# Seven second products from layer 2's first block pair on, and a second weight that is converted and summed within layer 1

## The chip, the cores and the metric

The kernel runs on one core of a Trainium2 chip. The metric is the device time of one execution in microseconds (us). Engines are named as in the profile: PE is TensorE (PEld its weight loads), DVE VectorE, ACT ScalarE, POOL GpSimd, SP the engine that issues most DMAs.

## The reference

A channel attention over 6016 tokens of 256 channels, then two dense layers with a hidden width of 2048:

```
s = kn.T @ qn / tau;  a = softmax(s);  x = v @ a          # a is 256 x 256
h = x @ w_in;   g = h * clip(h + 3, 0, 6) / 6;  x = g @ w_out      # layer 1
h = max(x @ w_in2, 0);  out = (h * h) @ w_out2                      # layer 2
```

The weights are 256 x 2048 and 2048 x 256 and come as 64-bit words. Inputs x, q, k and v and the output are float32.

## The kernel before

**Products.** All values are kept to float32 by splitting each operand into a high and a low part of a shorter type (`F32R`). One product of a 128 x 128 weight block with up to 512 tokens is therefore three matmuls: high x high, low x high, high x low.

**Tiling.** Tokens run along the free axis. They are cut into six block pairs (`pairs`), five of 2 x 512 and one of 2 x 448 tokens. The hidden width is cut into eight groups (`g`) of 2 x 128. `groups` lists layer, pair and group in the order of work: 2 x 6 x 8 = 96; groups 0 to 47 are layer 1, 48 to 95 layer 2. In a group, the first weight (2 x 2 blocks) meets the tokens (2 x 2 blocks), the result goes through the nonlinear function, and its split parts (`g` or `gs`) meet the second weight (2 x 2 blocks again). A 2 x 2 block product takes eight products in the plain way, or seven by sums of operands.

**Two schemes.** In the older one, `first7` does the first product in seven products and `second` the second product in eight, so a group has 21 + 24 = 45 matmuls; `hidden` does the nonlinear function and the split; results add up in four PSUM banks (`acc`). In the newer one, `first7s` does the first product in seven, and `items_direct` and `items_t` the second in seven, 42 matmuls. For this, sums of the hidden values are needed: `chain` adds two on VectorE and hands others to accumulating DMAs on GpSimd's queue (`move`, L1692), and `split_t` splits them three groups later. The second weight needs sums of its blocks too: `sums2` forms them from a converted block, four of 128 x 128, and splits them (`w2x`). Before the change, the newer scheme holds for layer 2 from its second pair on (`by7`, `S2SET`), except the last two groups of all, and group 56 is its first.

**Weights.** A second weight's block is loaded raw and converted by `pair_of`: six instructions on VectorE, two on ScalarE. Within layer 1, other work runs beside the groups, as listed in a table of group numbers: `make_w1` converts and sums layer 2's first weight and stores it to DRAM, `make_wo2` converts blocks 0 to 3 of its second weight and stores them (`wo2_d`). `load_wo2` brings those back once layer 1 is done with the buffer; blocks 4 to 7 are loaded raw and converted into their place (`need_wo(1, late)`) at the layer border. `sums2` runs in the eight groups of layer 2's first pair, one block each, in buffers that the layer-1 work has given up (`extra_cells`). First weights are loaded two groups ahead from DRAM, three buffers in turn (`load_w1`); from the newer scheme on, such a load also waits until a `move` has landed.

**Order.** Nothing is issued directly: each step is an `Op` with an engine, a cost, a delay and dependencies. PE and DMA operations keep the order in which the program adds them. For DVE, ACT and POOL, `Plan.run` picks by a rank: the latest time by which an operation must start for PE not to wait. `blame` raises ranks where the planned PE idles, for operations from `plan.settled` on. All SP transfers share one queue, and a transfer that waits holds up those behind it.

Of the kernel before, what the change touches and what calls it, by code (L numbers as in the profile page):

```python
# [196 lines left out]
def tile_kernel(  # L197
# [54 lines left out]
    PLAIN = 1  # L252

# [541 lines left out]
    def tokens(l, pr, parts=False):  # L795
# [696 lines left out]
    S2SET = {pr: tuple(range(NG if pr < NP - 1 else NG - 2)) for pr in range(1, NP)}  # L1492
    S2ALL = sorted({g for gs in S2SET.values() for g in gs})
    S2AT = {g: g + 3 for g in range(NG)}

    def by7(l, pr, g):
        return l == 1 and g in S2SET.get(pr, ())

# [24 lines left out]
    def sums2(k, g):  # L1523

        t, free = {}, cv_r.take()
        p = wo[1, g]

        def f_a():
            em = cv_p.tile([P, 2, 512], F32, tag="em", name="a2")
            t["a"], t["s"] = em[:, 0], em[:, 1].rearrange("p (k n) -> p k n", n=P)  # L1530
            V.tensor_tensor(
                t["a"], p["hl"][:, :512].bitcast(F32), p["hl"][:, 512:].bitcast(F32), ALU.add
            )

        def a(e, i):
            c = i * C + e * P
            return t["a"][:, c : c + P]

        def f1():
            V.tensor_tensor(t["s"][:, 0], a(1, 0), a(1, 1), ALU.subtract)  # L1540

        def f2():
            V.scalar_tensor_tensor(t["s"][:, 1], t["s"][:, 0], -1.0, a(0, 1), ALU.mult, ALU.subtract)

        def f3():
            V.tensor_tensor(t["s"][:, 2], a(0, 1), a(1, 1), ALU.subtract)

        def f4():
            V.tensor_tensor(t["s"][:, 3], a(0, 0), t["s"][:, 1], ALU.add)

        cell = cells["x", k]

        def f_hi():
            A.activation(cell.ap()[:, 0], t["s"], AF.Copy)

        def f_lo():
            x = cell.ap()
            V.tensor_tensor(x[:, 1], t["s"], x[:, 0].bitcast(F32), ALU.subtract)

        c = dve_us(P)  # L1560
        o = ordered("cv", add("DVE", dve_us(512), f_a, wo_done[1, g], free))
        wo_held[1, g].append(o)
        s1 = add("DVE", c, f1, o)
        s2 = add("DVE", c, f2, s1)
        s3 = add("DVE", c, f3, o)
        s4 = add("DVE", c, f4, s2)
        hi = add("ACT", act_us(512), f_hi, s3, s4, cell.take())
        lo = add("DVE", dve_us(512), f_lo, hi)
        cv_r.reader(lo)
        w2x[g], w2x_done[g] = cell, (hi, lo)  # L1570

    def extra_cells():
        deps = all_of(op8_r)
        for k in range(2):
            cells["x", k] = Cell(lambda: pools["op8"].tile([P, 2, 4, P], F32R, tag="op8", name="w2x"), deps)
        deps = all_of(wA_r)
        for k in range(2, 6):
            cells["x", k] = Cell(lambda: wA.tile([P, 2, 4, P], F32R, tag="wA", name="w2x"), deps)

        for k in (6, 7):  # L1580
            cells["x", k] = Cell(lambda k=k: more_p.tile([P, 2, 4, P], F32R, tag=f"w2x{k}", name="w2x"))
# [41 lines left out]
    def first7s(pr, g):  # L1623

        l, n = 1, pairs[pr][1]
# [5 lines left out]
        u = {"n": n, "pr": pr, "g": g, "seven": seven, "R": R}  # L1631
# [139 lines left out]
    def second_of(u, bank, operand, w, w_ok, first=None, last=True):  # L1771

        n, (c, hi, lo) = u["n"], operand
        key = (u["pr"], bank)
# [3 lines left out]
        held = wo_held[1, u["g"]]  # L1778
# [48 lines left out]
    def items_t(u):  # L1827
        g = u["g"]
        return (
            lambda: second_of(u, "P7", u["t3"], w_sum(g, 2), w2x_done[g]),  # L1830
            lambda: second_of(u, "P6", u["t2"], w_sum(g, 1), w2x_done[g]),
            lambda: second_of(u, "P4", u["t4"], w_plain(g, 1, 0), wo_done[1, g]),
        )

    def items_direct(u):
        g, ok = u["g"], wo_done[1, u["g"]]
        return (
            lambda: second_of(u, "P2", u[3], w_plain(g, 0, 0), ok),
            lambda: second_of(u, "P3", u[2], w_sum(g, 3), w2x_done[g]),
            lambda: second_of(u, "P1", u[1], w_plain(g, 0, 1), ok),  # L1840
            lambda: flush(u, "f5", second_of(u, "Y", u["t1"], w_sum(g, 0), w2x_done[g], first=True)),
        )

    def items_plain(u):
        g, ok = u["g"], wo_done[1, u["g"]]

        def unit(k, e, bank, **kw):
            return lambda: second_of(u, bank, u[k], w_plain(g, e, ROW[k]), ok, **kw)
# [16 lines left out]
    def out_s(pr, e, b, src, op, held):  # L1865
        o, n = pairs[pr]

        queue = nc.scalar if pr == NP - 1 and e == b else nc.sync

        def f_st():  # L1870
            c = o + b * n
            queue.dma_start(outT[e * P : (e + 1) * P, c : c + n], src()[:, :n])

        def store():
            held.append(add("DMA", 0.73, f_st, op, lat=5.0))

        if pr == NP - 1:
# [13 lines left out]
    def dve_out(pr, dst, a, b, op, deps, order=None):  # L1891
        n = pairs[pr][1]
# [7 lines left out]
    def finish_a(pr):  # L1900
        n = pairs[pr][1]
# [21 lines left out]
    def finish_b(pr):  # L1923
# [8 lines left out]
        n = pairs[pr][1]  # L1932
# [17 lines left out]
    def finish_last(pr, z):  # L1950
        s1, f5, fz = cells["s1"], cells["f5"][pr % 2], cells["fz"]
        n = pairs[pr][1]
# [29 lines left out]
    groups = [(l, pr, g) for l in range(2) for pr in range(NP) for g in range(NG)]  # L1982

# [3 lines left out]
    for i, job in (  # L1987
        (16, ("w1", 0)), (20, ("wo2", 0)), (22, ("w1", 1)), (27, ("wo2", 1)), (29, ("w1", 2)),
        (34, ("wo2", 2)), (36, ("w1", 3)), (41, ("wo2", 3)),
    ):  # L1990
# [13 lines left out]
    for i, (l, pr, g) in enumerate(groups):  # L2004
        if l == 0 and pr == 0:
            stores.pop(0)()
        k = i - (NP + 1) * NG
# [12 lines left out]
        for _ in range(1 if l and pr else len(pending)):  # L2020
# [20 lines left out]
        if g == (0 if l else 2) and i + NG < len(groups):  # L2041
            x_load = tokens(*groups[i + NG][:2], l == 1 and pr > 0)
            if not (l and pr):
                list(x_load)
        if l and pr and g < 7 and pr < NP - 1:
# [11 lines left out]
        if k >= 0:  # L2057
            steps, us[k] = first7s(pr, g)
# [10 lines left out]
            elif d:  # L2069
# [4 lines left out]
                if (pr, g) == (NP - 1, NG - 1):  # L2074
# [39 lines left out]
    finish_last(pr, x[7])  # L2114
# [3 lines left out]
    finish_rest(pr)  # L2118
# [48 lines left out]
```

## Time and profile before

| | |
|---|---|
| time, median of 3 runs | 1019.07 us (1018.51 to 1019.6) |
| profiled execution | 1017.72 us, its span 1015.8 us |
| PE busy | 1007.2 us, 4508 matmuls |
| DVE / ACT / POOL busy | 886.8 / 791.6 / 100.4 us |
| DMA | 188.73 MB, mean 186 GB/s |
| granted clock | 1.00 |

The span runs from the first to the last instruction. A busy PE is not a PE at its peak, since the rows of neighbouring matmuls overlap; its turn is the distance from one start to the next. Layer 2's first pair runs from 547.3 to 628.39 us, and the newer scheme's first matmul is at 628.39 us.

### The profile page before, as it was taken

What the parts mean: (1) busy time and instruction counts of PE and PEld (TensorE: products, weight loads), DVE (VectorE), ACT (ScalarE), POOL (GpSimd) and SP (SyncE); (2) the same over time, 40 slices, a digit from 0 to 9 for tenths busy, and PEclk for the clock granted to TensorE, in tenths of its full rate; (3) what the DMA queues carried; (4) which work ended last, traced back from release to release, by engine and by line L of the source; (5) the groups of instructions that cost most, each with busy time, mean ns of one, the idle gap of its engine ahead of it and who ended that gap; (6) DMA issues with size and microseconds to landing.
All of it is one profiled execution on the core that took longest, in us unless ns stands there. A gap on an engine that the chain in (4) does not pass through costs nothing.

```text
span 1015.8 us, 12950 instructions
## 1 busy us (share of the span) xinstructions
PE 1007.2 (99%) x4508; PEld 842.7 (83%) x4508; DVE 886.8 (87%) x1350; ACT 791.6 (78%) x1190; POOL 100.4 (10%) x97
## 2 busy tenths in 40 slices
PE   9999999999999999999999999999999999999998
PEld 7888888888888888888998888888888788888897
DVE  3999987988989899799788998789999889999886
ACT  5787667677778778777767888889889788888884
POOL 3400000000000000000000000122222222222220
PEclk9999999999999999999999999999999999999999
DMA  9657536536463744653755423697997888897892
GB/s 363 268 177 247 151 120 196 193 130 215 148 207 114 244 135 134 219 171 126 252 195 195 145 75 118 173 219 170 223 220 182 186 225 197 194 231 196 189 221 70
DMA packets 70208, 188.73 MB, mean 186 GB/s; under 512 B 7296, under 2 KB 11648, under 8 KB 68864
## 3 DMA queue, kind: packets, MB, share of 16 engines
q1 hardware_dynamic: 54048, 158.16, 46.3%
q0 software_dynamic: 15808, 29.30, 17.2%
q8 instruction: 35, 0.57, 0.2%
q10 hardware_dynamic: 288, 0.46, 0.1%
q14 instruction: 29, 0.24, 0.1%
HBM read 126.35 MB, written 32.24 MB: 156 GB/s over the span
## 4 chain that ended last, share of the span: by engine, by line
PE 81%; DMA 10%; issue 4%; DVE 3%; POOL 1%; ACT 0%; SPq 0%; DVEq 0%; POOLq 0%
PE acc L1419 9%; PE acc L1420 9%; PE acc L1425 9%; PE A L1327 4%; PE xy L1640 4%; PE A L1328 4%; PE A L1326 4%; PE xy L1642 4%; PE xy L1641 4%; PE s L958 3%; DMA rs<-rs 3%; DMA rc<-rc 2%; PE acc L1783 2%; PE acc L1784 2%; PE acc L1785 2%
## 5 line engine op out<-in xcount | busy, mean ns | idle before, releaser
L1419 PE MATMUL acc<-g,wo 128*128 128x512 f32 (+1 forms) x448 | 172.9, 386 | 0.0
L1420 PE MATMUL acc<-g,wo 128*128 128x512 f32 (+1 forms) x448 | 172.9, 386 | 0.0
L1208 ACT ACTIVATE g<-r 128x1024 fp32r<-128x1024 f32 (+1 forms) x112 | 117.1, 1046 | 46.1 <-DVE r L1182 45.2
L1212 DVE TENSOR_TENSOR g<-r,g 128x1024 fp32r<-128x1024 f32 (+1 forms) x112 | 135.0, 1206 | 20.0 <-ACT g L1208 19.3
L1425 PE MATMUL acc<-g,wo 128*128 128x512 f32 (+1 forms) x448 | 136.6, 386 | 0.0
L1420 PEld LDWEIGHTS acc<-g,wo 128*128 128x128 f32 x448 | 84.1, 188 | 16.2
L1419 PEld LDWEIGHTS acc<-g,wo 128*128 128x128 f32 x448 | 84.1, 188 | 16.2
L1425 PEld LDWEIGHTS acc<-g,wo 128*128 128x128 f32 x448 | 84.1, 188 | 16.1
L1692 POOL DMA_DIRECT2D rs<-rs x20 | 21.2, 1060 | 665.4 <-DVE gs L1676 619.4
L1177 ACT ACTIVATE r<-hp,three 128x1024 f32<-128x1024 f32 (+1 forms) x40 | 45.3, 1132 | 43.8 <-DVE hp L1359 43.5
L1351 ACT ACTIVATE hp<-A 128x512 f32<-128x512 f32 (+1 forms) x96 | 56.6, 590 | 12.9 <-PE A L1328 11.9
L1640 PE MATMUL xy<-xt,w 128*128 128x512 f32 (+1 forms) x160 | 62.4, 390 | 0.0
L1642 PE MATMUL xy<-xt,w 128*128 128x512 f32 (+1 forms) x160 | 61.6, 385 | 0.0
L1641 PE MATMUL xy<-xt,w 128*128 128x512 f32 (+1 forms) x160 | 61.6, 385 | 0.0
L1182 DVE SCALAR_TENSOR_TENSOR r<-r,hp 128x1024 f32<-128x1024 f32 (+1 forms) x40 | 47.9, 1198 | 14.8 <-ACT r L1177 14.3
L1359 DVE TENSOR_TENSOR hp<-B,hp 128x512 f32<-128x512 f32 (+1 forms) x48 | 32.6, 680 | 20.5 <-PE B L1328 15.0
L1640 PE MATMUL xy<-xb,w 128*128 128x512 f32 (+1 forms) x120 | 46.4, 387 | 0.7 <-ACT hs L1665 0.6
L1783 PE MATMUL acc<-gs,wo 128*128 128x512 f32 (+1 forms) x122 | 46.9, 384 | 0.0
L1785 PE MATMUL acc<-gs,wo 128*128 128x512 f32 (+1 forms) x122 | 46.9, 384 | 0.0
L1784 PE MATMUL acc<-gs,wo 128*128 128x512 f32 (+1 forms) x122 | 46.9, 384 | 0.0
L1676 DVE TENSOR_TENSOR gs<-rs,gs 128x512 fp32r<-128x512 f32 (+3 forms) x50 | 43.7, 880 | 3.4 <-ACT gs L1671 3.0
L1642 PE MATMUL xy<-xb,w 128*128 128x512 f32 (+1 forms) x120 | 46.2, 385 | 0.0
(388 smaller groups left out, 2776.4 us busy)
## 6 DMA issues: line engine op xcount, KB each, us to landing
w<-w1d SPq DMA_DIRECT2D x176, 448.0 KB, 4.4
qk<-in_qk_dram SPq DMA_DIRECT2D x8, 1024.0 KB, 16.6
w1d<-wA SPq DMA_DIRECT2D x16, 448.0 KB, 5.6
xr<-in_vT_dram SPq DMA_DIRECT2D x5, 1024.0 KB, 7.2
x2d<-o SPq DMA_DIRECT2D x20, 256.0 KB, 3.5
w1d<-wA SPq DMA_DIRECT2D x16, 256.0 KB, 2.5
rs<-rs POOLq DMA_DIRECT2D x8, 512.0 KB, 6.1
rp<-rp POOLq DMA_DIRECT2D x8, 512.0 KB, 6.1
```

Source lines behind the costliest of these rows:

```text
L1208: A.activation(t["g"][:, a:b, 0, :n], t["t"][:, a:b, :n], AF.Copy)
L1212: V.tensor_tensor(g[:, a:b, 1, :n], t["t"][:, a:b, :n], g[:, a:b, 0, :n].bitcast(F32), ALU.subtract)
L1351: A.activation(dst(), t[bank][:, :n], AF.Copy)
L1419: T_.matmul(acc[b, e][:, :n], w(e, 0), gh_, start=first_of, stop=False)
L1420: T_.matmul(acc[b, e][:, :n], w(e, 1), gh_, start=False, stop=False)
L1425: T_.matmul(acc[b, e][:, :n], w(e, 0), gl_, start=False, stop=last_of_b)
L1640: T_.matmul(ps, wh, xh, start=start, stop=False, skip_group_check=True)
L1641: T_.matmul(ps, wl, xh, start=False, stop=False, skip_group_check=True)
L1642: T_.matmul(ps, wh, xl, start=False, stop=True, skip_group_check=True)
L1783: T_.matmul(ps, wh, gh, start=first, stop=False, skip_group_check=True)
L1784: T_.matmul(ps, wl, gh, start=False, stop=False, skip_group_check=True)
L1785: T_.matmul(ps, wh, gl, start=False, stop=last, skip_group_check=True)
```

## The change

The newer scheme starts with layer 2 (`FIRST = (1, 0, 0)`), at group 48 instead of 56. All eight blocks of layer 2's second weight are now converted within layer 1 (`JOBS`, groups 13 to 39 instead of 16 to 41), stored, and loaded back at groups 42 to 49. The sums of blocks 0 to 3 are formed right after their conversion, from the converted block and before it is given up; those of blocks 4 to 7 at groups 48 to 51, two groups after their load, the last three of them in the buffers `fz` and `s1`. `sums2` now works in place, in half a buffer. Tokens of layer 2's second pair come in four pieces. Functions of the newer scheme get the layer as an argument, so that the pair's number counts through both layers. `SOME` is empty: layer 1 stays as it was.

```diff
+    FIRST = (1, 0, 0)
+    JOBS = (
+        (13, ("w1", 0)), (16, ("wo2", 0)), (18, ("wo2", 1)), (20, ("w1", 1)), (23, ("wo2", 4)),
...
+    GAP = 2
@@ make_wo2
+        if i < 4:
+            if i == 2:
+                extra_cells((2, 3), op8_p, "op8", op8_r)
+            sums2(1, i, (p, (hi, lo), wA_held))
@@ tokens
-        for k in (1, 0, 3, 2) if l and pr else range(4):
+        for k in (1, 0, 3, 2) if fast(l, pr) else range(4):
@@
-    S2SET = {pr: tuple(range(NG if pr < NP - 1 else NG - 2)) for pr in range(1, NP)}
+    groups = [(l, pr, g) for l in range(2) for pr in range(NP) for g in range(NG)]
+    K0 = groups.index(FIRST)
+    LAG = 3
     def by7(l, pr, g):
-        return l == 1 and g in S2SET.get(pr, ())
+        if groups.index((l, pr, g)) < K0:
+            return False
+        return g in SOME if l == 0 else pr < NP - 1 or g < NG - 2
@@ sums2
-    def sums2(k, g):
+    def sums2(l, g, early=None):
+        (p, ready, read), held = early or (wo[l, g], wo_done[l, g], wo_held[l, g]), []
+        if "fz" in cells:
+            tmp = cells[("fz", "s1")[g % 2]]
+        else:
+            tmp = Cell(lambda: cv_p.tile([P, 2, 512], F32, tag="em", name="a2")[:, 0], cv_r.take())
@@ the loop over groups
-        k = i - (NP + 1) * NG
+        k = i - K0
-        late = i - (NP - 1) * NG - 2
-        if 0 <= late < NG // 2:
+        late = i - (NP - 1) * NG - (2 if K0 == NP * NG else 4)
+        if 0 <= late < NG:
             load_wo2(late)
-        elif NG // 2 <= late < NG:
-            need_wo(1, late)
-        if -NG <= k < 0:
-            if k == -NG:
-                extra_cells()
-            if k == -6:
-                plan.settled = len(plan.ops)
-            sums2(k + NG, S2ALL[k + NG])
+        if k == -5:
+            extra_cells(range(4, NG), wA, "wA", wA_r)
+        if k == -6:
+            plan.settled = len(plan.ops)
+        if 4 <= late - GAP < NG:
+            sums2(1, late - GAP)
```

PE at the layer border, from the last product of layer 1's last group (`A057`) on. Before, the older scheme goes on with layer 2's first group:

```order
L1328 MATMUL A057_4766<-xb22_4147,w1_4617 128x448
L1326 MATMUL A100_4854<-xb11_4488,w1_4693 128x512
L1327 MATMUL A100_4854<-xb11_4488,w1_4693 128x512
L1328 MATMUL A100_4854<-xb11_4488,w1_4693 128x512
L1326 MATMUL C100_4862<-xb21_4510,w1_4693 128x512
L1327 MATMUL C100_4862<-xb21_4510,w1_4693 128x512
L1328 MATMUL C100_4862<-xb21_4510,w1_4693 128x512
```

After, the newer scheme (`xy` banks) starts there, with the second products of layer 1's last group (`acc05..`) between:

```order
L1340 MATMUL A057_4853<-xb22_4233,w1_4701 128x448
L1661 MATMUL xy_4941<-xb11_4655,w1_4780 128x512
L1662 MATMUL xy_4941<-xb11_4655,w1_4780 128x512
L1663 MATMUL xy_4941<-xb11_4655,w1_4780 128x512
L1431 MATMUL acc0500_4363<-g_4935,wo07_1267 128x448
L1432 MATMUL acc0500_4363<-g_4935,wo07_1267 128x448
L1661 MATMUL xy_4957<-xb21_4660,w1_4780 128x512
L1662 MATMUL xy_4957<-xb21_4660,w1_4780 128x512
L1663 MATMUL xy_4957<-xb21_4660,w1_4780 128x512
```

Up to that row PE's order is the same in both, and in all it has 4373 rows before and 4349 after.

SP in the middle of layer 1, where blocks of the second weight pass (`wo21r` is block 1 raw, `wo2d1` its store; `w1` from `w1d..` the first weights of a coming group, `win2..` raw first weights of layer 2). Before:

```order
L330 DMA wo21r_3110<-in_w_out2_dram 128x512
L585 DMA w1_3158<-w1d06_115 128x896 x2
L585 DMA w1_3241<-w1d07_116 128x896 x2
L500 DMA wo2d1_102<-wA_3214 128x1024
L330 DMA win220r_3281<-in_w_in2_dram 128x512
L330 DMA win221r_3289<-in_w_in2_dram 128x512
L585 DMA w1_3322<-w1d00_109 128x896 x2
L585 DMA w1_3408<-w1d01_110 128x896 x2
```

After, blocks 4 and 5 pass in about the same groups, and block 1 has had its turn earlier:

```order
L508 DMA wo2d4_105<-wA_3074 128x1024
L338 DMA wo25r_3101<-in_w_out2_dram 128x512
L597 DMA w1_3119<-w1d04_113 128x896 x2
L814 DMA xr04_3138<-in_vT_dram 128x2x1024
L597 DMA w1_3157<-w1d05_114 128x896 x2
L508 DMA wo2d5_106<-wA_3204 128x1024
L338 DMA win220r_3255<-in_w_in2_dram 128x512
L338 DMA win221r_3269<-in_w_in2_dram 128x512
L597 DMA w1_3282<-w1d06_115 128x896 x2
L597 DMA w1_3303<-w1d07_116 128x896 x2
L597 DMA w1_3370<-w1d00_109 128x896 x2
```

There are now eight such stores instead of four, each with first weights of coming groups behind it, and SP has 294 rows for 283 in all.

DVE in layer 2's first pair before, where sums (`a2`, L1531 to L1549) and their low parts (`w2x`, L1558) stand between the steps of a group (`hp`, `h`, `r`, `g`):

```order
L1531 TENSOR_TENSOR a2_5313<-wo2_4602 128x512
L1359 TENSOR_TENSOR hp_5319<-C105_5315,hp_5319 128x512
L1540 TENSOR_TENSOR a2_5313<-a2_5313 128x128
L1531 TENSOR_TENSOR a2_5333<-wo3_4639 128x512
L1212 TENSOR_TENSOR g_5328<-r_5288,g_5328 128x2x512
L1543 SCALAR_TENSOR_TENSOR a2_5313<-a2_5313 128x128
L1546 TENSOR_TENSOR a2_5313<-a2_5313 128x128
L1549 TENSOR_TENSOR a2_5313<-a2_5313 128x128
L1540 TENSOR_TENSOR a2_5333<-a2_5333 128x128
L1558 TENSOR_TENSOR w2x_5349<-a2_5277,w2x_5349 128x512
L1359 TENSOR_TENSOR hp_5319<-B105_5323,hp_5319 128x512
```

DVE after, around the newer scheme's first totals (`ISA`), with the sums of block 4 and the low part of block 3 between:

```order
L1194 SCALAR_TENSOR_TENSOR r_4928<-r_4928,h_4888 128x448
L1224 TENSOR_TENSOR g_4935<-r_4913,g_4935 128x2x448
L1194 SCALAR_TENSOR_TENSOR r_4928<-r_4928,A057_4853 128x448
L1556 TENSOR_TENSOR a2_4955<-wo4_4803 128x512
L1561 TENSOR_TENSOR a2_4955<-a2_4955 128x128
L1679 ISA rs_4951<-xy_4957,rs_4951 128x512
L1224 TENSOR_TENSOR g_4961<-r_4928,g_4961 128x2x448
L1564 TENSOR_TENSOR a2_4955<-a2_4955 128x128
L1579 TENSOR_TENSOR w2x_4675<-a2_4575,w2x_4675 128x512
L1679 ISA rs_4973<-xy_4941,rs_4973 128x512
L1567 SCALAR_TENSOR_TENSOR a2_4955<-a2_4955 128x128
```

The sums of blocks 0 to 3 have been formed in layer 1 by then, and the totals and splits of the newer scheme stand where the older scheme's steps were.

## Rows read from the trace of the kernel before

**Rows 1.** The page, busy us (share of the span) and instructions by engine.

```profile
PE 1007.2 (99%) x4508; PEld 842.7 (83%) x4508; DVE 886.8 (87%) x1350; ACT 791.6 (78%) x1190; POOL 100.4 (10%) x97
```

**Rows 2.** TensorE's waits, whole span: us in total, times, longest.

```profile
PE xy L1640 <- ACT hs L1665: 0.6, 1, 0.6
PE A L1327 <- DMA w<-w1d: 0.2, 1, 0.2
```

**Rows 3.** TensorE's timeline, first matmul of groups: start us, us.

```profile
556.99 0.39 PE L1326 MATMUL A<-xb,w 128*128 128x512 f32 x1
...
567.19 0.39 PE L1326 MATMUL A<-xb,w 128*128 128x512 f32 x1
...
720.85 0.39 PE L1640 MATMUL xy<-xb,w 128*128 128x512 f32 x1
...
730.37 0.39 PE L1640 MATMUL xy<-xb,w 128*128 128x512 f32 x1
```

**Rows 4.** Stretches: length, then busy us by engine, in three pairs of each layer.

```profile
core 0: us, PE busy (x) PEld busy (x) DVE busy (x) ACT busy (x) POOL busy (x), PEclk, DMA share, GB/s
227.20:309.00 81.80, 81.80 (x363) 67.73 (x362) 72.71 (x107) 61.17 (x86) 0.00 (x0) 1.00 0.52 177
309.00:391.00 82.00, 82.00 (x364) 67.89 (x363) 75.43 (x110) 62.49 (x87) 0.00 (x0) 1.00 0.49 164
391.00:473.00 82.00, 82.00 (x364) 67.94 (x363) 73.56 (x112) 60.77 (x85) 0.00 (x0) 1.00 0.49 162
547.30:628.39 81.09, 81.09 (x362) 67.55 (x360) 74.70 (x131) 68.26 (x97) 0.00 (x0) 1.00 0.38 129
628.39:704.70 76.31, 76.31 (x335) 61.96 (x334) 63.93 (x89) 66.98 (x107) 13.98 (x13) 1.00 0.77 191
704.70:781.10 76.40, 76.40 (x338) 62.84 (x337) 70.31 (x101) 66.47 (x104) 16.84 (x16) 1.00 0.86 203
```

**Rows 5.** VectorE's instructions of one conversion and of the sums: min/median/max ns.

```profile
L391 DVE TENSOR_SCALAR em<-wo23r x1: 416/416/416, 499.8 to 499.8; 128x512 uint32<-128x512 uint32 x1
...
L412 DVE SCALAR_TENSOR_TENSOR em<-wo23r,em x1: 684/684/684, 504.5 to 504.5; 128x512 f32<-128x512 uint32 x1
...
L1531 DVE TENSOR_TENSOR a<-wo x8: 680/684/685, 565.8 to 615.0; 128x512 f32<-128x512 f32 x8
...
L1546 DVE TENSOR_TENSOR a<-a x8: 282/284/287, 571.7 to 620.8; 128x128 f32<-128x128 f32 x8
```

**Rows 6.** VectorE's timeline, two neighbours.

```profile
791.40 0.68 DVE L1676 TENSOR_TENSOR gs<-rs,gs 128x512 fp32r<-128x512 f32 x1
792.00 0.69 DVE L1676 TENSOR_TENSOR gs<-hs,gs 128x512 fp32r<-128x512 f32 x1
```

**Rows 7.** ScalarE's and TensorE's timeline around the one loss in layer 2.

```profile
804.95 1.06 ACT L1671 ACTIVATE gs<-rs 128x1024 fp32r<-128x1024 f32 x1 [2.35 <-DMA rs<-rs]
...
797.20 0.39 PE L1640 MATMUL xy<-xb,w 128*128 128x512 f32 x1
...
807.49 0.50 PE L1640 MATMUL xy<-xb,w 128*128 128x512 f32 x1 [0.57 <-ACT hs L1665]
...
818.08 0.39 PE L1640 MATMUL xy<-xb,w 128*128 128x512 f32 x1
```

**Rows 8.** SP's queue: a wait, its timeline, a transfer's us to landing, TensorE.

```profile
SPq L500 <- DVE wA L416: 19.6, 4, 11.2
...
513.01 0.32 SPq L500 DMA_DIRECT2D wo2d<-wA  x1
...
513.90 1.27 SPq L585 DMA_DIRECT2D w<-w1d  x2
...
w<-w1d SPq DMA_DIRECT2D x176, 448.0 KB, 4.4
...
528.68 0.37 PE L1326 MATMUL A<-xb,w 128*128 128x448 f32 x1
```

**Rows 9.** Accumulating transfers of one buffer, to landing.

```profile
DMA to landing us min/median/max: 4.2/5.7/8.9
```

More of the change, by code (lines that the diff above doesn't have):

```diff
@@ L1521, in all_of @@
         return [ring.take() for _ in range(ring.bufs)]
-    def sums2(k, g):
[L1525 to L1533, printed above, removed]
+    def sums2(l, g, early=None):
+        if ("x", g) not in cells:
+            more_cell(g)
+        (p, ready, read), held = early or (wo[l, g], wo_done[l, g], wo_held[l, g]), []
[3 more added lines that the diff above has]
+            tmp = Cell(lambda: cv_p.tile([P, 2, 512], F32, tag="em", name="a2")[:, 0], cv_r.take())
+            held = cv_r.last
@@ L1566, in sums2 @@
-        s4 = add("DVE", c, f4, s2)
-        hi = add("ACT", act_us(512), f_hi, s3, s4, cell.take())
-        lo = add("DVE", dve_us(512), f_lo, hi)
[L1569 to L1581, printed above, removed]
+        o = add("DVE", dve_us(512), f_a, ready, tmp.take())
@@ new lines, in sums2, with more_cell, extra_cells @@
+        if "fz" not in cells:
+            ordered("cv", o)
+        read.append(o)
+        for f in (f1, f2, f3, f4):
+            o = add("DVE", c, f, o)
+        hi = add("ACT", act_us(512), f_hi, o, cell.take())
+        lo = add("DVE", dve_us(512), f_lo, hi)
+        held.append(lo)
+        tmp.use(lo)
+        w2x[l, g], w2x_done[l, g] = cell, (hi, lo)
+    def more_cell(g):
+        cells["x", g] = Cell(lambda: more_p.tile([P, 2, 4, P], F32R, tag=f"w2x{g}", name="w2x"))
+    def extra_cells(gs, pool, name, ring):
+        deps = all_of(ring)
+        for g in gs:
+            cells["x", g] = Cell(lambda: pool.tile([P, 2, 4, P], F32R, tag=name, name="w2x"), deps)
@@ L1863, in tile_kernel, with out_s @@
     outs = {}
-    def out_s(pr, e, b, src, op, held):
-        o, n = pairs[pr]
-        queue = nc.scalar if pr == NP - 1 and e == b else nc.sync
+    def out_s(q, e, b, src, op, held):
+        o, n = pairs[q % NP]
+        queue = nc.scalar if q == 2 * NP - 1 and e == b else nc.sync
         def f_st():
             c = o + b * n
-            queue.dma_start(outT[e * P : (e + 1) * P, c : c + n], src()[:, :n])
+            if q < NP:
+                nc.sync.dma_start(x2_d[q][:, e, b * n : (b + 1) * n], src()[:, :n])
+            else:
+                queue.dma_start(outT[e * P : (e + 1) * P, c : c + n], src()[:, :n])
         def store():
             held.append(add("DMA", 0.73, f_st, op, lat=5.0))
-        if pr == NP - 1:
+            if q < NP:
+                x2_stored[q].append(held[-1])
+        if q == 2 * NP - 1:
             store()
@@ L1891, in dve_out @@
     def dve_out(pr, dst, a, b, op, deps, order=None):
-        n = pairs[pr][1]
+        n = pairs[pr % NP][1]
         def f():
@@ L1900, in finish_a @@
     def finish_a(pr):
-        n = pairs[pr][1]
+        n = pairs[pr % NP][1]
         s1 = cells["s1"]
@@ L1931, in finish_b @@
         c22, held = new_o("c22")
-        n = pairs[pr][1]
+        n = pairs[pr % NP][1]
         def f_c22():
@@ L1951, in finish_last @@
         s1, f5, fz = cells["s1"], cells["f5"][pr % 2], cells["fz"]
-        n = pairs[pr][1]
+        n = pairs[pr % NP][1]
         s = add(
@@ L1995, in tile_kernel @@
     us, due, rest = {}, {}, {}
-    for pr, gs in S2SET.items():
-        for g in gs:
-            due[NG * (pr - 1) + S2AT[g]] = NG * (pr - 1) + g
+    for k, key in enumerate(groups[K0:]):
+        if by7(*key):
+            due[k + LAG] = k
     REST = ((1, 0, 1, 0, 1, 2, 3), (1, 0, 1, 0, 0, 0, 0), (1, 0, 1, 0, 0, 0, 0))
@@ L2019, in tile_kernel @@
             us[k - 2]["chain4"]()
-        for _ in range(1 if l and pr else len(pending)):
+        for _ in range(1 if k >= 0 else len(pending)):
             if pending and len(us) - pending[0][0] >= HOLD:
```

106 lines of the change are left out of this document (55 added, 51 removed).

## The prediction

> **What bounds the kernel now.** I read the page's busy shares first, then TensorE's list of waits, then its timeline at group starts, then the stretches. TensorE is busy for 1007.2 of 1015.8 us [rows 1]. That share alone says little, since a matmul's row lasts longer than its turn; the waits say it better: after the load phase TensorE waits 0.6 us for a square and 0.2 us for a weight load, and nothing else [rows 2]. So the time is the number of matmuls times their turn. A 512-column matmul's turn comes out of the timeline: in layer 2's first block pair a group starts at 556.99 and the next at 567.19, 10.20 us for 21 first and 24 second matmuls, 0.2267 us each; later a group takes 720.85 to 730.37, 9.52 us for 21 and 21, again 0.2267 us [rows 3]. The granted clock is 1.00 in every stretch [rows 4]. VectorE, at 886.8 us, is the engine with the least room [rows 1]; its busy time in the stretches is what the added work has to fit into [rows 4].
>
> **The change part by part.**
>
> *Matmuls removed.* The eight groups of layer 2's first pair get seven second products of three matmuls instead of eight; the order of TensorE has 4349 rows for 4373 and is the same up to layer 2's first group. 24 x 0.2267 = 5.44 us. The two group lengths give the same: (10.20 - 9.52) x 8 = 5.44 us. All of it is on the path, because TensorE waits for nothing in this stretch: 81.09 us busy of 81.09 [rows 4].
>
> The Trainium skill (TensorE: Matmul & The Clock Gate, "Back-to-back issue gap") gives about 131 ns per 512-column matmul in a stream with weight loads, and 216 ns for the lone gap; by these the 24 matmuls would be worth 3.1 or 5.2 us. The trace shows 226.7 ns, above both, and by the trace it is 5.44.
>
> *Conversion and sums moved into layer 1.* Four more blocks of layer 2's second weight are converted there. VectorE's part of one block is three instructions of 0.416 us and three of 0.684 us [rows 5], 3.30 us. Four blocks also get their sums early: 0.684, four of 0.284 and another of the first kind, 2.50 us each. By durations that is 4 x 3.30 + 4 x 2.50 = 23.2 us; but neighbours overlap (one of 0.68 us starts at 791.40, the next at 792.00, so a turn is 0.60 [rows 6]), and with 0.08 less on each of 48 instructions it is 19.4 us. ScalarE gets two instructions per block and has more room, 62.49 us busy of 82.00 in the fullest pair [rows 4]. The work falls into the groups from 13 to 43, some 300 us. In three block pairs of that stretch VectorE is busy for 72.71, 75.43 and 73.56 of 245.8 us [rows 4], so 24.1 us are free there, and more before and after. A quarter of 19.4 us per pair would bring the fullest pair from 75.43 to 80.3 of 82.0. That is tight, but only totals that TensorE needs stand ahead in the planner's rank, and a conversion has several groups to be done in. Low end 0. High end: each of the 12 long conversion instructions of 0.684 us stands right ahead of a total that TensorE is waiting for, 8.2 us. The nearest row is the pair at 75.43 of 82, 92% full, in which TensorE loses nothing; I take 0.
>
> *Layer 2's first pair in the other scheme.* There VectorE drops four conversions and at least four sums, and runs the groups of the later pairs instead: 70.31 busy of 76.40 us in a full pair and 63.93 of 76.31 in the first one, whose early groups lack the late products; it was 74.70 of 81.09 [rows 4]. ScalarE goes from 68.26 of 81.09 to about 66.98 of 76.31. Four sums are left in this pair (10.0 us at most by durations): 63.9 + 10.0 = 73.9 of 76.3. The three of them that come last use buffers free until the first outputs are finished.
>
> *The hand-over* between the schemes moves from the pair border at 628.39 to the one between the layers at 547.3. Before, TensorE waits for nothing there: it is busy for all of the 76.31 us that follow [rows 4]. Low end 0, high end the dearest loss the scheme shows anywhere, 1.8 us (next paragraph); I take 0.
>
> *Sixteen more accumulating transfers*, two per group, on GpSimd's queue. They take 4.2 to 8.9 us to land, 5.7 in the middle [rows 9]. ScalarE runs in order, so a late one holds up the squares behind the split that waits for it. That is the one real loss of the scheme: ScalarE idles 2.35 us until 804.95 for such a transfer, and TensorE's groups start at 797.20, 807.49 and 818.08 [rows 7], 20.88 us for two where 19.04 is normal, 1.84 us lost. One such loss in five pairs makes 0.4 us for one pair more. Low end 0, high end two of them, 3.7 us; I take 0.4.
>
> *SP's queue* loses four loads of raw weight and gains them back earlier, with four stores and four loads of a converted block more, and the second pair's tokens come in four pieces. A store waits for the last instruction of its conversion, and behind it stand the first weights of coming groups. In four stores SP waited 19.6 us, once 11.2 [rows 8]. That once, the store went at 513.01 and the weight load behind it at 513.90; it lands in 4.4 us, at 518.3, and is read at 528.68 [rows 8]: 10.4 us to spare. Low end 0; high end: see the third rival; I take 0.
>
> *Sum:* -5.44 + 0.4 = -5.0 us. The profiled execution took 1017.72 us, 1015.8 of it span and 1.9 around it; that gives 1012.7. The median of the runs shown, 1019.07, is 1.35 above it, so the forecast is **1014.1 us**.
>
> **The rivals.**
>
> *The existing loss goes too.* All transfers and splits of layer 2 are put in order anew, and the late one at 805 may no longer hit a full ScalarE. For it: one such loss only, where four pairs run alike, so it hangs on a detail of the order. Against it: DMA engines are as full as before, 0.86 of their time in a full pair [rows 4]. Time: 1019.07 - 5.44 - 1.84 = 1011.8.
>
> *Late transfers eat the gain.* The first pair had its DMA engines 0.38 busy; in the scheme it will be 0.77 [rows 4], and now at a time when converted weights, tokens and the last stores of layer 1 are under way too. Two to three losses of 1.84 us in the added pair and at the hand-over: 1019.07 - 5.44 + 4.6 = 1018.2, between 1017.3 and 1019.2. Against it: at 628.39 the same start went without a wait. The Trainium skill (DMA: Bandwidth & Descriptors, "Issuing engines are not separate DMA queues") says that transfers issued from GpSimd and SP run on the same 16 engines and interleave; by that rule alone this would be the forecast, and the trace bears it out in one loss over five pairs.
>
> *SP stuck behind a conversion: slower.* In layer 1 VectorE has less room than before, and four more stores stand in SP's queue. If one waits 10.4 us longer than the 11.2 seen, 21.6 us, the next weights come late, and TensorE waits for all of what is beyond. It costs more than the change gains from 21.6 + 5.44 / 4 = 23.0 us per store on. At 24 us each: 4 x 2.4 - 5.44 = +4.2, 1023.2. Against it: the mean wait at these stores is 4.9 us (19.6 / 4), and in the fullest pair TensorE lost nothing.
>
> That the change doesn't do what it says is ruled out by the order, which has the 24 matmuls less.
>
> **How the numbers follow.** Forecast 64%, of its own range 1013.0 to 1015.6 (0 to 1.5 us of loss, and the scatter of the median, about 0.5); the existing loss gone too 13%; late transfers 15%; SP stuck 8%. A change of under 0.2%, 2.0 us, can't be told from none. Forecast and first rival lie clear of that, the second is inside it in two cases of three, the third mostly beyond it on the other side. Faster 0.64 + 0.13 + 0.05 = 0.82, same 0.11, slower 0.07. The range leaves out the third rival and the dear half of the second: 1011.6 to 1017.8.
>
> **What would show it right or wrong.** Right: 4484 matmuls for 4508; group starts in layer 2's first pair 9.5 us apart; no wait of TensorE between 100 us and the layer border; VectorE's busy time per pair of layer 1 up by some 5 us at an unchanged length of 82 us. Wrong: a wait of TensorE for a weight load in layer 1 (third rival), or for a square or a snapshot in the first ten groups of layer 2, with ScalarE idle until a transfer lands (second rival).

## The result and the profile after

The changed kernel is slower: 1023.17 us in the median of 11 runs (1021.19 to 1028.1) against 1017.38 of 11 runs of the kernel before beside it (1016.48 to 1021.01), a ratio of 1.0053, 95% interval 1.0038 to 1.0069. The forecast had been 5 us faster. The execution that was profiled is the longest, 1028.1 us, 4.9 above the median, so its losses are up to some 5 us too large in sum.

The page of the kernel after, busy time by engine (beside [rows 1]):

```profile
PE 1010.0 (98%) x4484; PEld 839.4 (82%) x4484; DVE 907.1 (88%) x1388; ACT 796.0 (78%) x1213; POOL 117.2 (11%) x113
```

The 24 matmuls are gone (4484 for 4508). TensorE's waits, whole span (us in total, times, longest; [rows 2] had two lines):

```profile
PE xy L1661 <- ACT rp L1673: 2.4, 2, 1.5
PE xy L1661 <- ACT rc L1673: 2.3, 3, 1.5
...
PE xy L1661 <- ACT hs L1673: 1.2, 1, 1.2
PE A L1339 <- DMA w<-w1d: 1.2, 2, 0.6
...
PE xy L1661 <- DVE r L1194: 0.6, 1, 0.6
PE A L1338 <- DMA w<-w1d: 0.4, 1, 0.4
```

Most are new waits for ScalarE's copies of first products (L1673) in layer 2; 1.6 us are for first weights in layer 1, and 0.6 for the border of the layers. The stretches (columns as in [rows 4]): a pair of layer 1, then layer 2's first, second, fourth and fifth pair:

```profile
226.00:308.00 82.00, 82.00 (x363) 67.93 (x362) 79.42 (x123) 63.97 (x89) 0.00 (x0) 1.00 0.52 183
550.10:626.60 76.50, 73.84 (x323) 59.51 (x322) 66.01 (x104) 64.11 (x103) 13.97 (x13) 1.00 0.76 192
626.60:704.10 77.50, 77.50 (x338) 62.18 (x337) 72.10 (x104) 67.04 (x106) 16.83 (x16) 1.00 0.86 204
782.50:861.10 78.60, 76.97 (x338) 62.57 (x337) 69.59 (x100) 65.97 (x104) 17.07 (x17) 1.00 0.84 201
861.10:942.30 81.20, 79.51 (x337) 63.53 (x337) 70.49 (x102) 67.03 (x107) 16.66 (x16) 0.98 0.81 193
```

Layer 1 takes its extra work nearly without a loss: VectorE is 79.42 us busy in a pair that still takes 82.00. Layer 2's first pair is shorter, 76.5 for 81.09 (323 matmuls for 362, the second products of its last groups now fall into the next pair; 323 turns of 0.2267 us are 73.2 us). But the later pairs, in which the change altered no instruction of the scheme, have grown from 76.4 to as much as 81.2. From TensorE's first matmul of layer 2 to its last it is 471.7 us, where it was 463.9. ScalarE's waits for the accumulating transfers, whole span, first of the kernel before:

```profile
ACT gs L1671 <- DMA rs<-rs: 3.7, 2, 2.3
ACT gs L1671 <- DMA rc<-rc: 0.4, 2, 0.3
ACT gs L1671 <- DMA rp<-rp: 0.3, 1, 0.3
```

and of the kernel after:

```profile
ACT gs L1692 <- DMA rs<-rs: 11.0, 7, 3.0
ACT gs L1692 <- DMA hs<-hs: 7.3, 7, 2.4
ACT gs L1692 <- DMA rc<-rc: 3.9, 4, 2.0
```

4.4 us have become 22.2. The dearest group shows how. Each group issues a move of 512 KB (the row of 1.20 us on GpSimd) and, once that has landed, one of 256 KB (0.90 us). GpSimd's timeline of the kernel after, then ScalarE's, then TensorE's first matmul of the group, the wait in it and the first matmul of the next group (beside [rows 7]):

```profile
879.20 1.20 POOL L1713 DMA_DIRECT2D rs<-rs  x1 [4.05 <-DVE gs L1697]
886.12 1.23 POOL L1713 DMA_DIRECT2D rp<-rp  x1 [5.73 <-DVE gs L1697]
888.03 0.91 POOL L1713 DMA_DIRECT2D rs<-rs  x1 [0.68 <-DMA rs<-rs]
...
887.64 1.06 ACT L1692 ACTIVATE gs<-rs 128x1024 fp32r<-128x1024 f32 x1 [1.85 <-DMA rs<-rs]
...
895.59 0.63 ACT L1692 ACTIVATE gs<-rs 128x512 fp32r<-128x512 f32 x1 [2.98 <-DMA rs<-rs]
...
890.18 0.50 PE L1661 MATMUL xy<-xb,w 128*128 128x512 f32 x1
...
896.75 0.50 PE L1661 MATMUL xy<-xt,w 128*128 128x512 f32 x1 [1.52 <-ACT rc L1673]
...
903.92 0.39 PE L1661 MATMUL xy<-xb,w 128*128 128x512 f32 x1
```

The large move of `rs` lands 8.4 us after its issue (879.20 to 887.64). The next group's large move, of `rp`, goes out at 886.12, ahead of the small one of `rs` at 888.03, which then takes 7.6 us. ScalarE, in order, stands 1.85 and 2.98 us; the copies of products behind it come late; the group takes 13.74 us for 9.52 (some 1.8 us of that is TensorE's clock, see the last section). Such a pair, in which the next group's large move goes ahead of this group's small one, I call turned. The kernel after has six. At each of them the small move lands after 6.2 to 8.0 us (median of all small moves 5.2), and ScalarE stands 0.7 to 3.0 us for it, 10.2 of the 22.2 us; the rest it stands for other moves that land late. The kernel before has one turned pair. Its large move goes out at 796.01, and GpSimd's next two rows are the next group's large move and this group's small one:

```profile
803.00 1.20 POOL L1692 DMA_DIRECT2D rp<-rp  x1 [5.79 <-DVE gs L1676]
805.28 0.90 POOL L1692 DMA_DIRECT2D rs<-rs  x1 [1.08 <-DMA rs<-rs]
```

That is the 1.84 us loss of [rows 7].

SP's wait at the stores of the converted blocks (beside [rows 8]), after:

```profile
SPq L508 <- DVE wA L424: 69.3, 8, 14.0
```

The landing of one buffer's moves (beside [rows 9]), after:

```profile
DMA to landing us min/median/max: 4.7/6.2/8.7
```

There are eight such stores now for four. Moves of this buffer land some 0.5 us later in the middle, but over all four buffers the middle hardly moves: 5.9 us before and 6.0 after for large moves, 5.2 in both for small ones. What grows is the number of late ones: eight large moves take over 7.6 us, where two did.

### The profile page after: what moved, and what is told of

Its sections match the earlier page's. It is cut to its first block, busy times and chain, and to the rows that moved or that the text cites. A ratio compares the mean times of both kernels' runs of the same rounds, so it can differ in the third digit from the quotient of the medians.

```text
span 1026.3 us, 13038 instructions
## 1 busy us (share of the span) xinstructions
PE 1010.0 (98%) x4484; PEld 839.4 (82%) x4484; DVE 907.1 (88%) x1388; ACT 796.0 (78%) x1213; POOL 117.2 (11%) x113
## 4 chain that ended last, share of the span: by engine, by line
PE 69%; DMA 15%; issue 7%; DVE 5%; ACT 2%; POOL 1%; SPq 0%; DVEq 0%; POOLq 0%; ACTq 0%
PE acc L1432 8%; PE acc L1437 8%; PE acc L1431 8%; PE xy L1661 4%; PE xy L1663 4%; PE xy L1662 4%; DMA hs<-hs 3%; PE A L1339 3%; DMA rc<-rc 3%; PE A L1340 3%; PE A L1338 3%; DMA qk<-in_qk_dram 3%; DMA rs<-rs 2%; PE acc L1804 2%; PE acc L1806 2%
## 5 line engine op out<-in xcount | busy, mean ns | idle before, releaser
L1431 PE MATMUL acc<-g,wo 128*128 128x512 f32 (+1 forms) x384 | 148.0, 385 | 0.0
L1432 PE MATMUL acc<-g,wo 128*128 128x512 f32 (+1 forms) x384 | 148.0, 385 | 0.0
L1220 ACT ACTIVATE g<-r 128x1024 fp32r<-128x1024 f32 (+1 forms) x96 | 100.1, 1042 | 36.2 <-DVE r L1194 35.9
L1224 DVE TENSOR_TENSOR g<-r,g 128x1024 fp32r<-128x1024 f32 (+1 forms) x96 | 115.4, 1202 | 13.4 <-ACT g L1220 13.0
L1437 PE MATMUL acc<-g,wo 128*128 128x512 f32 (+1 forms) x384 | 116.8, 385 | 0.0
L1431 PEld LDWEIGHTS acc<-g,wo 128*128 128x128 f32 x384 | 72.1, 188 | 13.7
L1437 PEld LDWEIGHTS acc<-g,wo 128*128 128x128 f32 x384 | 72.1, 188 | 13.7
L1432 PEld LDWEIGHTS acc<-g,wo 128*128 128x128 f32 x384 | 72.1, 188 | 13.6
L1661 PE MATMUL xy<-xt,w 128*128 128x512 f32 (+1 forms) x192 | 76.5, 399 | 5.9 <-ACT rp L1673 2.4
L1663 PE MATMUL xy<-xt,w 128*128 128x512 f32 (+1 forms) x192 | 74.6, 389 | 0.0
L1662 PE MATMUL xy<-xt,w 128*128 128x512 f32 (+1 forms) x192 | 74.6, 388 | 0.0
L1697 DVE TENSOR_TENSOR gs<-rs,gs 128x512 fp32r<-128x512 f32 (+3 forms) x60 | 52.6, 883 | 6.7 <-ACT gs L1692 6.4
L1661 PE MATMUL xy<-xb,w 128*128 128x512 f32 (+1 forms) x144 | 56.4, 392 | 1.5 <-DVE r L1194 0.6
L1692 ACT ACTIVATE gs<-rs 128x512 fp32r<-128x512 f32 (+3 forms) x60 | 47.0, 786 | 13.0 <-DMA rs<-rs 11.0
L1804 PE MATMUL acc<-gs,wo 128*128 128x512 f32 (+1 forms) x146 | 56.5, 387 | 0.0
L1806 PE MATMUL acc<-gs,wo 128*128 128x512 f32 (+1 forms) x146 | 56.5, 387 | 0.0
L1805 PE MATMUL acc<-gs,wo 128*128 128x512 f32 (+1 forms) x146 | 56.5, 387 | 0.0
L1194 DVE SCALAR_TENSOR_TENSOR r<-r,hp 128x1024 f32<-128x1024 f32 (+1 forms) x40 | 47.9, 1196 | 9.6 <-ACT r L1189 9.2
L1697 DVE TENSOR_TENSOR gs<-rc,gs 128x512 fp32r<-128x512 f32 (+3 forms) x58 | 51.1, 884 | 5.7 <-ACT gs L1692 5.5
L1662 PE MATMUL xy<-xb,w 128*128 128x512 f32 (+1 forms) x144 | 55.6, 386 | 0.0
```

What stands on the lines that cost most here:

```text
L1220: A.activation(t["g"][:, a:b, 0, :n], t["t"][:, a:b, :n], AF.Copy)
L1224: V.tensor_tensor(g[:, a:b, 1, :n], t["t"][:, a:b, :n], g[:, a:b, 0, :n].bitcast(F32), ALU.subtract)
L1431: T_.matmul(acc[b, e][:, :n], w(e, 0), gh_, start=first_of, stop=False)
L1432: T_.matmul(acc[b, e][:, :n], w(e, 1), gh_, start=False, stop=False)
L1437: T_.matmul(acc[b, e][:, :n], w(e, 0), gl_, start=False, stop=last_of_b)
L1661: T_.matmul(ps, wh, xh, start=start, stop=False, skip_group_check=True)
```

## The experiments

Each was timed beside the kernel before, on the same chip, in five rounds; intervals are 95%. Different experiments ran on different chips, so it is the ratios to the kernel before that are compared, and a difference of two ratios is uncertain by some 2 us.

**The moves in order.** The planner chooses GpSimd's order by rank; here it is kept as written, in the changed kernel and, as a control, in the one before:

```diff
-        in_order = {"PE": [], "DMA": []}
-        ready = {"DVE": [], "ACT": [], "POOL": []}
+        in_order = {"PE": [], "DMA": [], "POOL": []}
+        ready = {"DVE": [], "ACT": []}
...
-        at = {"PE": 0, "DMA": 0}
+        at = {"PE": 0, "DMA": 0, "POOL": 0}
```

Expected of the changed kernel: 

> The changed kernel, with the accumulating transfers on GpSimd's queue held in program order (a group's third-sum transfer always ahead of the next group's first one; the planner had turned this round six times, and once in the kernel before). Theory S (the turned pairs cost the gain): 1013 to 1016 us, against some 1017.4 before. Rival D (transfers land later than planned wherever they stand): 1020 to 1023 us, as the change. Rival L (the loss is made in layer 1, by the weight loads behind the new stores): 1020 us or more.

Expected of the control: 

> The kernel before, with the accumulating transfers in program order; it had one turned pair. Theory S: its one loss of 1.8 us goes, 1015.5 us. Rival D: no change, 1017.4 us. Rival L says nothing.

Measured: 1016.91 us, 0.9981 (0.9970 to 0.9993) of the kernel before, and 1016.61 us, 0.9978 (0.9966 to 0.9990), for the control. So the changed kernel loses 1.0053 - 0.9981 = 0.72%, 7.3 us, with its turned pairs, and the kernel before 2.2 us with its one. With GpSimd's order the planner's order of the other engines changes too (in the changed kernel another instruction stands at 217 of VectorE's 1388 places and at 238 of ScalarE's 1213), so these are prices of the turned pairs together with the order around them. Theory S fits: it expected 0.9957 to 0.9986 of the kernel before, though its time, 1016 us at most, is missed by 0.9; rivals D and L, at 1020 us or more, are out. But the two kernels are now level, and the 5.44 us of matmuls are still missing.

**The second weight alone.** The newer scheme starts at layer 2's second pair again; the second weight is still converted and summed within layer 1:

```diff
-    FIRST = (1, 0, 0)
+    FIRST = (1, 1, 0)
-    GAP = 2
+    GAP = 3
```

Expected: 

> The changed kernel with the newer scheme from layer 2's second pair on, as before; the conversion of all eight blocks and four of the sums stay in layer 1 (the other sums one group later). It has one turned pair, as the kernel before. Theory S and rival D: 1016.5 to 1018.5 us. Rival L: 1020 us or more, with waits of TensorE for weight loads in layer 1.

Measured: 1.0000 (0.9987 to 1.0014). What was moved into layer 1 costs nothing that can be told, with an interval of 1.4 us to either side; most of the loss comes with the newer scheme's earlier start.

**A longer landing in the plan.** The planner is told that moves land 1.5 us later, first with GpSimd's order free, then with it kept, in both kernels; last by 0.6 us with the order kept:

```diff
-  lat=(MOVE_LAT, 6.0)[size - 1])          # 4.4 and 6.0
+  lat=(MOVE_LAT + 1.5, 7.5)[size - 1])    # the last: (MOVE_LAT + 0.6, 6.6)
```

Expected, order free: 

> The changed kernel, with the planner told that an accumulating transfer lands 1.5 us later (5.9 and 7.5 instead of 4.4 and 6.0 us). The plan puts the splits later, and turns some 18 pairs on GpSimd's queue instead of six. Theory S: 1025 us or more. Rival D: 1012 to 1017 us, since the splits then come when the transfers have landed.

Expected, order kept: 

> The changed kernel with GpSimd's moves kept in their written order, and the planner told that a move lands 1.5 us later than it assumed (5.9 and 7.5 us in place of 4.4 and 6.0). Theory D (in order, 6.6 us of TensorE's time are still lost because 512 KB moves land 8.3 to 9.7 us after their issue while the plan has ScalarE split them 6.5 us after): ScalarE no longer stands in front of late splits, and the time falls from 1016.9 to 1011 to 1014 us. Theory H (the rest is lost elsewhere, at the hand-over of layer 1 to layer 2 and in layer 1): within 1 us of 1016.9.

Expected of the control: 

> The same two edits in the kernel before: the control for the run above. Its TensorE lost only about 1 us to waits with the moves in order, so both theories expect 1015.5 to 1017 us; theory D then has the changed kernel 3 to 5.4 us under it, theory H has the two level.

Expected, 0.6 us: 

> The changed kernel with the moves in order, the planner told 5.0 and 6.6 us for a move's landing, about the medians measured (4.7 to 5.8 and 5.9 to 6.6) in place of 4.4 and 6.0; 5.9 and 7.5 had cost 4 us. Theory D': fewer late splits at a smaller price in the plan, 0.995 to 0.998 of before. Rival (the plan has no room for a longer landing, each tenth of a us is paid in its own order): 0.999 to 1.002.

Measured: 1.0037 (1.0026 to 1.0048) with the order free, where the plan turned 17 pairs; 1.0024 (1.0011 to 1.0037) with it kept, 1.0034 (1.0020 to 1.0049) for the control, 1.0006 (0.9994 to 1.0017) by 0.6 us. The first three fit neither theory, the last fits the rival. ScalarE's waits for moves did vanish with the order kept, 0.6 us for 8.9; but the time rose by 0.4%. TensorE's longest waits are then for the low parts split by VectorE (`C L1806`, 1.6 us in three). Why a plan with later splits runs longer than that explains was not settled. Neither of the two allowances bought off the late landings.

**Smaller loads beside the moves.** In the in-order kernel, GpSimd's, SP's and ScalarE's timelines around the dearest wait:

```profile
790.00 0.91 POOL L1713 DMA_DIRECT2D rc<-rc  x1 [4.56 <-DMA rc<-rc]
795.09 1.20 POOL L1713 DMA_DIRECT2D rs<-rs  x1 [4.19 <-DVE gs L1697]
...
789.68 6.16 SPq L597 DMA_DIRECT2D w<-w1d  x2
795.89 0.43 SPq L819 DMA_DIRECT2D xr<-x2d  x1
...
804.82 1.06 ACT L1692 ACTIVATE gs<-rs 128x1024 fp32r<-128x1024 f32 x1 [3.09 <-DMA rs<-rs]
```

SP's two rows of a weight load end at 795.84: the second half waits until the small move of 790.00 has landed, and so goes out 0.4 us after the next large move, with a token piece behind it. That move lands 9.7 us after its issue; ScalarE was there at 6.6. The cut (six sevenths of the low parts of the first weights, from layer 2's second pair on, are left out of the computation; the plan's order stays):

```diff
+                few = l == 1 and pr and h      # later: l == 1 and h;  l == 1 and pr
+                e = a + 1 if few else b
-                o.ins = nc.sync.dma_start(p["w"][:, h, : b - a].bitcast(F32), w1_d[l, g][:, h, a:b])
+                o.ins = nc.sync.dma_start(p["w"][:, h, : e - a].bitcast(F32), w1_d[l, g][:, h, a:e])
```

Expected of the changed kernel: 

> The changed kernel with the moves in order; from layer 2's second block pair on, each second half of a first weight (the low parts) is loaded as one seventh, 64 in place of 448 KB, and all first products of the group take that one slice as their low part (so seven eighths of the low parts are left out of the computation). The plan's order is the same. This half waits for the group's 256 KB move to land, which comes just after the next 512 KB move was issued, so it shares the DMA engines with that move. Theory D': the 512 KB moves then land in under 7 us, ScalarE stands before few of them, and the time is 1011 to 1014 us. Rival: the transfers beside them are not what makes them late; landings stay up to 9 us and the time stays within 1 us of 1016.9.

Expected of the control: 

> The kernel before with the moves in order and the same second halves cut to one seventh from layer 2's second pair on (the same part of the computation left out): the control. By theory D' little is left to gain, 1015 to 1016.6 us, and the changed kernel with the same cut lies 3 to 5 us under it; by the rival the two stay level.

Expected with the first pair cut too: 

> As the changed kernel in order with small second halves, now in layer 2's first pair too (seven eighths of the low parts of the first weights of layer 2 are left out of the computation). Theory D' has the 1.2 us that TensorE lost at 577 and 585 us for late moves in the first pair go as well: 0.993 to 0.995 of before, against 0.9951 with the first pair left as it was. Rival: the first pair's loss has another cause, 0.995 to 0.996.

Measured: 0.9951 (0.9935 to 0.9966); the control 0.9972 (0.9956 to 0.9987); with the first pair 0.9948 (0.9931 to 0.9965), no difference that can be told. The cut is worth 0.30% to the changed kernel, 3.1 us, and 0.06% to the one before; the time of the changed kernel, 1013.5 us, is in the range of theory D', but the distance between the two, 2.0 us, is below the 3 to 5 expected. Then both halves were cut, so that the other slices' values are left out too:

Expected of the changed kernel: 

> The changed kernel with the moves in order; from layer 2's second pair on both halves of each first weight are loaded as one seventh (128 in place of 896 KB a group; all first products of a group take that one slice, so the other slices' values are left out of the computation). The order of the plan is the same. Theory D' (the rest of the missing gain is moves that land late because other transfers share the DMA engines): with most of those gone the changed kernel keeps its 5.4 us less some 0.9 for late weights in layer 1 and 0.75 at the border to layer 2: 3 to 4.5 us under the kernel before with the same cut, at 0.993 to 0.995 of the kernel before. Rival (something else of the change costs 2 to 3 us more): within 2.5 us of the control.

Expected of the control: 

> The control: the kernel before with the moves in order and both halves cut to one seventh from layer 2's second pair on. Both theories: 0.9965 to 0.9985 of before, as with the second half alone cut (0.9972).

Measured: 0.9948 (0.9935 to 0.9961), 1012.33 us, and 0.9973 (0.9962 to 0.9984), 1015.59 us: 3.3 us apart by the medians, 2.5 by the ratios, where theory D' had 3 to 4.5 and the rival under 2.5: between the two. Layer 2's five full pairs of the in-order kernel (columns as in [rows 4]):

```profile
546.80:620.50 73.70, 73.10 (x323) 59.60 (x322) 66.46 (x104) 64.47 (x103) 13.99 (x13) 1.00 0.77 199
620.50:698.60 78.10, 77.74 (x338) 62.35 (x337) 71.71 (x104) 66.50 (x106) 16.86 (x16) 1.00 0.87 203
698.60:777.10 78.50, 77.38 (x338) 62.37 (x336) 69.99 (x100) 65.98 (x105) 16.94 (x16) 1.00 0.83 198
777.10:855.90 78.80, 77.41 (x336) 62.64 (x337) 70.02 (x100) 66.54 (x105) 16.89 (x16) 1.00 0.85 203
855.90:932.40 76.50, 76.50 (x338) 62.78 (x337) 69.65 (x100) 66.25 (x105) 16.95 (x16) 1.00 0.86 203
```

and of the same kernel with both halves cut:

```profile
547.70:621.90 74.20, 73.38 (x323) 59.61 (x322) 66.54 (x104) 64.47 (x103) 13.99 (x13) 1.00 0.74 183
621.90:698.60 76.70, 76.67 (x337) 62.62 (x336) 71.55 (x104) 66.43 (x106) 16.83 (x16) 1.00 0.62 125
698.60:775.10 76.50, 76.50 (x338) 62.78 (x338) 70.07 (x100) 66.33 (x105) 16.89 (x16) 1.00 0.61 124
775.10:851.50 76.40, 76.40 (x338) 62.73 (x337) 69.99 (x100) 66.23 (x105) 16.89 (x16) 1.00 0.62 125
851.50:927.90 76.40, 76.40 (x338) 62.74 (x337) 69.59 (x100) 66.23 (x105) 16.87 (x16) 1.00 0.61 124
```

With the DMA engines at 0.62 in place of 0.85, each pair after the first is at 76.4 to 76.7 us, eight groups of 9.52 and little else; VectorE and ScalarE do the same work in both. The fifth pair of the in-order kernel takes 76.5 us with its loads whole, at 0.86: the mean share alone doesn't make the loss. TensorE's two longest waits after the load phase in the cut kernel are for first weights in layer 1 (1.4 us in two) and 0.6 us at the border.

**Two other orders of the transfers, nothing left out.** First the token piece and the out store ahead of the second weight half; then the second half gated like the first:

```diff
-            w1_part(1, [t["move4"]] if gated else ())
...
+        if second_half:          # after the out store and the token piece
+            second_half()        # w1_part(1, [t["move4"]])
```

```diff
-            w1_part(1, [t["move4"]] if gated else ())
+            w1_part(1, [t["move"]] if gated else ())
```

Expected of the first: 

> The changed kernel with GpSimd's moves in order, and on SP's queue the token piece and the out store (256 KB each) ahead of the second weight half, which waits for the 256 KB move; so of 704 KB that went beside the next 512 KB move 448 KB are left, with nothing left out of the computation. Theory D' (what goes beside the 512 KB move makes it late; cutting 384 of 704 KB gave 3.0 us): some 2 us under the in-order kernel's 0.998 of before, 0.995 to 0.997 of before. Rival: only the weight half counts, or the pieces now delay the 256 KB moves as much: within 1 us of 0.998.

Expected of its control: 

> The kernel before with the moves in order and the same order on SP's queue (token piece and out store ahead of the second weight half), the control. Cutting the second half gave it 0.6 us, so both theories expect within 1 us of 0.998 of before; by theory D' the changed kernel with the same edits lies 2 us or more under it.

Expected of the second: 

> The changed kernel with the moves in order; the second weight half no longer waits for the 256 KB move, but for the 512 KB move as the first half does. So both halves (896 KB) and the token piece go beside the 256 KB move, and little is left beside the next 512 KB move. Theory D': 512 KB moves land in time, 0.994 to 0.997 of before. Rival (the 256 KB moves, planned at 4.4 us, now land late and stop ScalarE in their turn): above 1.000 of before.

Measured: 1.0012 (0.9999 to 1.0026), its control 1.0017 (1.0006 to 1.0029), and 1.0417 (1.0401 to 1.0433). The second is as its rival had it: what leaves the large move's side goes to the small one's. The first fits neither range (0.995 to 0.997, or within 1 us of 0.998); it is slower by 3 us than the in-order kernel, in the direction of its rival. Landing of one buffer's moves (size, median us) in the in-order kernel:

```profile
rs<-rs POOLq DMA_DIRECT2D x10, 512.0 KB, 6.2
rs<-rs POOLq DMA_DIRECT2D x10, 256.0 KB, 5.4
```

with both halves beside the small move:

```profile
rs<-rs POOLq DMA_DIRECT2D x10, 512.0 KB, 8.1
rs<-rs POOLq DMA_DIRECT2D x10, 256.0 KB, 7.4
```

and with both halves cut:

```profile
rs<-rs POOLq DMA_DIRECT2D x10, 512.0 KB, 5.5
rs<-rs POOLq DMA_DIRECT2D x10, 256.0 KB, 3.4
```

In the middle one 34% of the chain that ended last is DMA, against 17% in the in-order kernel and 4% in the cut one.

Of the kernels that leave nothing out, those in order are the fastest, 0.9981 and 0.9978 of before; the first of them beats both kernels of this case, and the change adds nothing to it that can be told.

## Why the prediction was wrong

**The step that failed** is the sixteen more accumulating transfers, costed at 0.4 us as "one such loss in five pairs makes 0.4 us for one pair more". It took the loss at 805 us as a rate per pair, and the other pairs' order as given. It was the mark of one turned pair, which GpSimd's order shows, and the planner dealt those out anew over all of layer 2. The prediction's first rival had the new order, but only as a gain. Shown: six turned pairs for one, 7.3 us with them, 2.2 before, net +5.1. Both signs of being wrong that it had named appeared: waits of TensorE for first weights in layer 1, and for ScalarE in layer 2's first groups, where ScalarE had stood idle until 580.98 and 601.96 us for a small move.

**What was undervalued beside it** is that moves land late because of the transfers beside them: in the in-order kernel large moves take 5.0 to 9.7 us, while ScalarE comes to a split as early as 6.6 us after the issue. The prediction's rival "late transfers eat the gain" had such waits, with two to three losses around the new pair; they stand in all pairs. The weight loads beside the moves cost the in-order kernel 0.9981 - 0.9948 = 3.4 us and the control 0.5, net +2.9, uncertain by 2.4. The Trainium skill (DMA: Bandwidth & Descriptors, "Issuing engines are not separate DMA queues") has transfers of GpSimd's queue and of SP's interleave on the same engines; the traces agree, 5.4 us for a small move with full loads beside it, 3.4 with small ones. But full engines are not what makes a large move late: while the five latest, of 8.0 to 9.7 us, were under way, the DMA engines were 0.51 to 0.70 busy, and they were 1.01 busy during one that landed in 6.4 us. The one of 9.7 us and that one, in the in-order kernel (columns as in [rows 4]):

```profile
795.10:804.80 9.70, 9.70 (x45) 7.86 (x44) 7.11 (x11) 6.28 (x10) 1.19 (x1) 1.00 0.60 130
774.90:781.30 6.40, 5.38 (x24) 4.10 (x23) 5.91 (x8) 6.40 (x12) 1.58 (x2) 1.00 1.01 219
```

So the loads are shown as the cause, by the cut, but not how they delay a move. Why loads of the same size hurt the changed kernel more than the one before, at the same places of the plan, stays open too: the large move at 795 us landed after 9.7 us in the one and 8.2 in the other, one execution each.

**The matmuls removed** were right: 24 fewer, and a steady group of 9.52 us. Of the 5.44 us, 2.5 to 3.3 show once turned pairs and loads are out of the way. In the profiles of the two kernels with both halves cut, layer 2 takes 458.4 us from first matmul to last with the change and 461.8 without.

**Conversion and sums in layer 1** were right in size (79.42 us of VectorE's time in a pair, forecast 80.3 for the fullest) and near in cost: 0, by the run with the second weight alone. But TensorE waits 1.6 us for first weights there in the profile after, and from its first second-product matmul to layer 2's first matmul it takes 483.0 us in the mean of eleven profiles with the work (482.0 to 483.6), 482.1 of six without (481.9 to 482.4): about 1 us. The **third rival** is its mechanism at a small price. In each of the eleven TensorE waits 0.6 to 0.8 us for a first weight at 491 to 495 us, and in none of the six. In the kernel after, SP stands 4.7 us at a second weight's store, and the loads behind it come late; SP's timeline, then TensorE's wait:

```profile
485.86 0.32 SPq L508 DMA_DIRECT2D wo2d<-wA  x1
...
486.77 1.27 SPq L597 DMA_DIRECT2D w<-w1d  x2
...
494.75 0.47 PE L1339 MATMUL A<-xb,w 128*128 128x448 f32 x1 [0.60 <-DMA w<-w1d]
```

That the store is the reason is read from the order of the rows, not tried apart. SP's wait at these stores grew from 19.6 to 69.3 us in eight, the longest 14.0, short of the 23.0 from which it would have decided. The other waits for first weights in layer 1, 0.43 and 0.63 us at 218.85 and 219.99 in the kernel after, are not new: all six kernels without the work wait there too, 0.2 to 1.4 us.

**The hand-over**, taken at 0 of 0 to 1.8 us, costs TensorE 0.6 us at 551 us, and 0.6 or 0.7 in each kernel that starts the newer scheme there, for a bank that VectorE still reads for layer 1's last group (L1194).

**The sum** of what was shown and read: -5.44 (matmuls) + 5.1 (turned pairs) + 2.9 (loads beside moves) + 1.0 (layer 1) + 0.6 (border) = +4.2, against 5.4 measured by the ratio. The two terms from runs are uncertain by more than 2 us each; some 1 us more is read off groups of the first pair in the cut kernel, 10.1 us for 9.52 at the worst, whose cause was not tried apart.

## What to carry to other kernels

A stall that shows once in a repeating pattern is not a rate: look up what stands in another order there, on the queues too, before you cost the next stretch by it; where a planner sets the order, an edit can deal such places out anew over the whole stretch. In a stage in which an engine that runs in order waits for transfers with others beside them, the price of more work is read from the landing times against the time at which the engine gets there, not from anyone's busy share. And the saving is seen first with the disturbance taken out of both kernels alike.

## What the hardware showed beside

After the wait of 1.52 us at 896.75, TensorE's granted clock fell to half, 1.2 for 2.4 GHz: matmuls start 0.43 us apart (898.32, 898.75) for 0.227, and 0.23 again from 900.74 on. The stretches in the kernel after:

```profile
894.00:896.70 2.70, 1.24 (x5) 0.48 (x3) 1.27 (x3) 1.11 (x3) 0.00 (x0) 1.00 0.64 109
...
898.00:900.00 2.00, 2.00 (x6) 1.55 (x5) 1.43 (x3) 1.17 (x3) 0.03 (x1) 0.50 0.94 305
```

Some nine matmuls at 0.2 us more each are 1.8 us, more than the wait itself; a wait of 1.3 us in the in-order kernel left the clock at 1.00 over its pair, and so did one of 2.8 us at 590.0 in the kernel with both halves beside the small move.
